# Per-head column tiles for the KV products, a sixteen-tile fold into the output weights, and a reordered opening, in an adaLN, linear-attention and SwiGLU block

## The chip, the cores and the metric

The kernel runs on one core of a Trainium2 chip. The metric is the device time of one execution in microseconds. A run also has a mean granted clock of the tensor engine (PE), 1.0 at full speed. All runs below count as fast (the single runs e7, e8 and e11 have no state), but in many of them the clock stood at half for some us near the start (3.4 or 6.8 us in the traces), which costs about 2 us (0.8 to 2.3 us in the traces). As the differences here are about as large, I use three readings: the medians, the runs with a clock of 1.000 alone ("full clock"), and distances between two instructions within a trace, which repeat to about 0.01 us.

## The reference, cut to what matters

```
S, D, H, Dh, F = 2048, 1024, 32, 32, 3584          # one sequence, bf16
mod = silu(c) @ w_mod -> sa, ca, ga, sb, cb, gb    # six rows of D
h   = layernorm(x) * (1 + ca) + sa
q, k, v = h @ wqkv                                 # 32 heads of 32
pq, pk  = phi(q), phi(k)                           # phi(t) = t+1 or exp(t), + 1e-6
kv = pk^T v  per head (32 x 32);  z = sum of pk per head
o  = (pq kv) / (pq z + 1e-6);     x = x + ga * (o @ wo)
h  = layernorm(x) * (1 + cb) + sb
x  = x + gb * ((silu(h @ w_gate) * (h @ w_up)) @ w_down)
```

## The kernel before

KV is the product `kv` of the reference, summed over all rows; a bank is one of the accumulators that PE writes. The sequence is cut into four chunks of 512 rows. Each chunk's key matmuls are eight groups of 8 matmuls (128x128 weights, 512 columns). After the first two key groups of a chunk come the KV products of the chunk before:

```python
def kv_phase(sc):
    for hg0 in range(0, HG, 3):                    # HG = 8 groups of four heads
        nh = min(3, HG - hg0)
        kvp = acc_b("kvp")                         # one bank for three groups
        ...
        for i in range(nh):
            for t in range(STC):                   # 4 tiles of 128 rows
                mm(kvv[:, i, :], lhsT=pks[sc][:, t, (hg0 + i) * P:(hg0 + i + 1) * P],
                   rhs=vs[sc][:, t, hg0 + i, 0:P + 1], start=(t == 0), stop=(t == STC - 1))
        ...                                        # added to kv_acc on VectorE
```

That is 128 keys by 128 values of four heads plus a column of ones, though only the four 32x32 blocks on the diagonal are wanted. A mask later zeroes the rest, eight transposes turn the masked groups, and sixteen matmuls, three after each query group, fold them into `wo`, so that attention and output projection become one product:

```python
        for hg, nb in wf[3 * (qc - 5):3 * (qc - 4)]:
            ps = acc_b("wf")
            w = wo[hg // 4][:, hg % 4, nb * NB:(nb + 1) * NB]
            mm(ps[:], lhsT=KVT[:, hg, :], rhs=w, start=True, stop=True)
            nc.scalar.copy(out=w, in_=ps[:])
```

Two chunks compute modulation rows directly behind `kv_phase`: `mod_rows`, 32 matmuls in four column tiles (32 weight columns each). The opening normalises the first chunk, transposes it on PE, and waits for the modulation weights `wme`. `keep_warm` issues dummy matmuls; `mod_block` computes shift or scale columns; `modulate` applies them on VectorE:

```python
        pe_transpose_tile(hT, xns[0], 0, DC)
        keep_warm(spare, 1)
        mod_block(0, 1, 0, 4)                      # scale
        pe_transpose_tile(hT, xns[1], 1, DC)
        keep_warm(spare, 1)
        pe_transpose_tile(hT, xns[2], 2, DC // 2)
        keep_warm(spare, 3)
        mod_block(0, 0, 0, 2)                      # shift, two columns
        for cc in (0, 1):
            modulate(hT, cc, ca1T, saT, 0, H)
        mod_block(0, 0, 2, 4)
        ...
        k_mms(0, gs, accs, 0, 3)                   # first key matmuls, six groups at once
        xn3 = ln1_norm(*ln1_stats(0, 3), dve=True) # fourth tile
        pe_transpose_tile(hT, xn3, 3, DC // 2)
        ...
        k_mms(0, gs7, accs7, 0, 4)                 # seventh key group
        mod_block(1, 0, 0, 2)
        for cc in (4, 5):
            modulate(hT, cc, ca1T, saT)
        k_mms(0, gs + gs7, accs + accs7, 4, 5)     # fifth chunk of the contraction
```

## Time and profile before

| reading | before |
|---|---|
| median (four runs beside the change) | 844.27 us (843.91 to 845.21) |
| profiled execution | 843.6 us, clock 1.000 |
| first key matmul to first value matmul | 17.08 us |
| first value matmul to first output projection | 151.66 us |
| PE time that one KV phase adds | 1.81 us, four of them |
| PE time that the fold matmuls add | 3.46 us |

The page of the kernel before: busy time of each engine, then PE's busy tenths and clock in 40 slices, then the chain of waits. (PEld is PE's weight loads, DVE is VectorE, ACT ScalarE, POOL GpSimd, SPq the queue of SyncE.)

```profile
PE 833.8 (99%) x4289; PEld 385.5 (46%) x4289; DVE 306.8 (36%) x599; ACT 176.2 (21%) x268; POOL 55.6 (7%) x163
...
PE   8999999999999999999999999999999999999998
...
PEclk9999999999999999999999999999999999999999
...
PE 98%; DMA 1%; SPq 0%; DVE 0%; issue 0%
```

PE is almost never free. The waits of the kernel before (what PE waited for, us in total, times, longest) name all there is, and all of it falls in the first 24 us:

```profile
PE mod_ps L98 <- DMA wme<-in_w_mod_dram: 1.8, 1, 1.8
PE acc L98 <- DVE sel L412: 1.2, 1, 1.2
PE acc L98 <- DVE hT L221: 0.7, 1, 0.7
PE mod_ps L98 <- DVE saT L267: 0.2, 1, 0.2
```

A matmul's shown duration includes its pipeline. What it costs PE is the distance between starts. The timeline of the kernel before (start, us, engine, line, matmul, array rows*columns, shape that streams, count; in brackets the idle time before and what ended it), KV and fold:

```profile
62.94 1.98 PE L98 MATMUL kvp<-v,pk 128*128 128x129 bf16 x32
64.75 10.52 PE L98 MATMUL acc<-wk,hT 128*128 128x512 bf16 x48
...
92.38 1.98 PE L98 MATMUL kvp<-v,pk 128*128 128x129 bf16 x32
94.29 1.91 PE L98 MATMUL modr<-wml,sc 128*32 128x512 bf16 x32
96.13 3.63 PE L98 MATMUL acc<-wk,hT 128*128 128x512 bf16 x16
...
162.23 0.63 PE L98 MATMUL den<-pq,Zden 128*32 128x128 bf16 x32
162.79 3.63 PE L98 MATMUL acc<-hT,wq 128*128 128x512 bf16 x16
166.25 0.81 PE L98 MATMUL wf<-wo,kvs 128*128 128x512 bf16 x3
166.90 1.89 PE L98 MATMUL acc<-hT,wq 128*128 128x512 bf16 x8
```

From 62.94 to 64.75 is the 1.81 us of a KV phase, 56.6 ns per matmul; three fold matmuls take 0.65 us, 216 ns each. The denominator matmuls (`den`, four column tiles) are the model for the new KV form: single starts there are 2 to 5 ns apart within a group of four, and the groups are 56 ns apart. The same timeline, the opening:

```profile
10.69 0.95 PE L98 MATMUL mod_ps<-scT,wme 128*128 128x1 bf16 x32 [1.83 <-DMA wme<-in_w_mod_dram]
...
13.55 0.55 PE L98 MATMUL mod_ps<-scT,wme 128*128 128x1 bf16 x16
14.36 0.54 PE L98 MATMUL mod_ps<-scT,wme 128*128 128x1 bf16 x16 [0.25 <-DVE saT L267]
14.78 4.06 PE L98 MATMUL acc<-wk,hT 128*128 128x512 bf16 x18
18.80 0.62 PE L101 MATMUL tp<-ident,xn 128*128 128x128 bf16 x8
...
23.46 2.55 PE L98 MATMUL acc<-wk,hT 128*128 128x512 bf16 x11 [0.71 <-DVE hT L221]
```

The first shift block at 13.55 us starts when its load lands (13.51 us), not when PE is ready.

### The profile page before, as it was taken

The page shows a single profiled execution, that of the slowest core. Times are in us where ns is not written, and L with a number is a line of the kernel's source. Part 1 is how long each engine was busy: PE and PEld are TensorE (multiplying, and loading weights), DVE is VectorE, ACT ScalarE, POOL GpSimd, SP SyncE. Part 2 cuts the span into 40 slices and gives each one's busy share as a digit, 9 for nine tenths or more (in the row PEclk, how much of TensorE's full clock was granted, in tenths as well). Part 3 has the DMA queues.
Part 4 walks back from the last instruction along what each step waited for, and adds up shares of the span by engine and source line. Part 5 has one row for each costly group of instructions (what it writes and reads, how often), then busy time and mean ns, then how long its engine had stood idle before and what let it go on. Part 6 is the DMA issues. An engine that isn't in the chain of part 4 may idle for free.

```text
span 841.5 us, 10528 instructions
## 1 busy us (share of the span) xinstructions
PE 833.8 (99%) x4289; PEld 385.5 (46%) x4289; DVE 306.8 (36%) x599; ACT 176.2 (21%) x268; POOL 55.6 (7%) x163
## 2 busy tenths in 40 slices
PE   8999999999999999999999999999999999999998
PEld 4444444544444444444444444444444444444444
DVE  5656563467523324432221344211124432111122
ACT  3355353354211111101111010111110101111000
POOL 3011010112050001100000010000001100000000
PEclk9999999999999999999999999999999999999999
DMA  9895770029998545528434073581504629720011
GB/s 304 308 248 122 232 188 1 2 52 250 348 236 251 193 145 175 154 70 257 151 100 150 25 233 106 178 260 52 198 1 131 182 69 315 238 66 1 17 60 50
DMA packets 127232, 128.74 MB, mean 153 GB/s; under 512 B 33616, under 2 KB 108880, under 8 KB 126672
## 3 DMA queue, kind: packets, MB, share of 16 engines
q1 hardware_dynamic: 123600, 115.36, 45.7%
q0 software_dynamic: 3584, 12.72, 4.9%
q8 instruction: 33, 0.54, 0.3%
q14 instruction: 15, 0.12, 0.1%
HBM read 108.01 MB, written 12.71 MB: 143 GB/s over the span
## 4 chain that ended last, share of the span: by engine, by line
PE 98%; DMA 1%; SPq 0%; DVE 0%; issue 0%
PE acc L98 89%; PE a_ps L98 7%; DMA wme<-in_w_mod_dram 1%; PE kvp L98 1%; PE modr L98 0%; PE wf L98 0%; PE mod_ps L98 0%; PE den L98 0%; SPq L120 0%; PE tp L101 0%; PE bcr L98 0%; SPq L131 0%; SPq L125 0%; DVE hT L221 0%; PE mcol L98 0%
## 5 line engine op out<-in xcount | busy, mean ns | idle before, releaser
L98 PE MATMUL acc<-h2T,wgu 128*128 128x512 bf16 x1792 | 387.6, 379 | 0.0
L98 PEld LDWEIGHTS <-wgu 128*128 128x128 bf16 x1792 | 175.0, 98 | 211.6
L98 PE MATMUL acc<-wd,gu 128*128 128x512 bf16 (+2 forms) x924 | 196.1, 373 | 0.0
L591 DVE TENSOR_TENSOR gu<-acc,e 128x512 bf16<-128x512 f32 x112 | 77.5, 692 | 299.3 <-PE acc L98 296.5
L590 ACT ACTIVATE e<-acc 128x512 f32<-128x512 f32 x112 | 66.9, 597 | 374.8 <-PE acc L98 374.8
L98 PEld LDWEIGHTS <-gu 128*128 128x128 bf16 x924 | 89.2, 98 | 104.6
L98 PEld LDWEIGHTS <-hT 128*128 128x128 bf16 x512 | 49.4, 98 | 60.3 <-DVE hT L221 1.3
L612 DVE TENSOR_TENSOR e<-acc,gb_bc 128x512 f32<-128x512 f32 (+2 forms) x33 | 22.3, 676 | 131.3 <-PE acc L98 131.3
L98 PE MATMUL acc<-wk,hT 128*128 128x512 bf16 x256 | 57.6, 379 | 0.7 <-DVE hT L221 0.7
L98 PE MATMUL a_ps<-wo,pq 128*128 128x512 bf16 x256 | 57.4, 379 | 0.0
L98 PE MATMUL acc<-hT,wq 128*128 128x512 bf16 x256 | 57.1, 379 | 0.0
L98 PE MATMUL acc<-wv,hT 128*128 128x512 bf16 x256 | 55.9, 379 | 0.0
L273 ACT ACTIVATE eb<-acc 128x512 bf16<-128x512 f32 x64 | 37.9, 596 | 63.4 <-PE acc L98 60.3
L218 ACT ACTIVATE xn<-x,nmr,rstd 128x1024 bf16<-128x1024 f32 x16 | 19.8, 1240 | 126.3 <-POOL nmr L216 126.3
L274 DVE TENSOR_SCALAR eb<-eb 128x512 bf16<-128x512 bf16 x64 | 18.4, 291 | 58.7 <-ACT eb L273 58.6
L98 PEld LDWEIGHTS <-pq 128*128 128x128 bf16 x256 | 25.0, 98 | 30.3
L98 PEld LDWEIGHTS <-wq 128*128 128x128 bf16 x256 | 24.9, 98 | 29.8
L559 POOL DMA_DIRECT2D x_scratch<-x x16 | 9.6, 600 | 418.6 <-DVE x L552 418.6
L552 DVE TENSOR_TENSOR x<-a_ps,x_sb 128x512 f32<-128x512 f32 x32 | 22.1, 692 | 8.2 <-PE a_ps L98 8.1
L202 POOL TENSOR_TENSOR rstd<-veps,neg_half 128x1 f32<-128x1 f32 x32 | 18.0, 562 | 86.0 <-DVE veps L200 75.2
L311 ACT CAST v<-acc 128x512 bf16<-128x512 f32 x32 | 18.3, 582 | 22.0 <-PE acc L98 22.0
L615 DVE TENSOR_TENSOR ob<-e,x1r 128x512 bf16<-128x512 f32 (+2 forms) x33 | 22.3, 675 | 1.0
(72 smaller groups left out, 276.9 us busy)
## 6 DMA issues: line engine op xcount, KB each, us to landing
wgu<-in_B_w_gate_dram SPq DMA_DIRECT2D x28, 1024.0 KB, 7.5
wgu<-in_B_w_up_dram SPq DMA_DIRECT2D x28, 1024.0 KB, 8.7
x_sb<-in_A_x_dram SPq DMA_DIRECT2D x32, 256.0 KB, 6.7
wml<-in_w_mod_dram SPq DMA_DIRECT2D x8, 1024.0 KB, 8.6
x_scratch<-x POOLq DMA_DIRECT2D x16, 512.0 KB, 3.1
x1r<-x_scratch SPq DMA_DIRECT2D x31, 256.0 KB, 2.9
wd<-in_B_w_down_dram SPq DMA_DIRECT2D x7, 1024.0 KB, 5.6
rbc<-rden_scratch POOLq DMA_DIRECT2D x16, 256.0 KB, 5.2
```

The lines of the kernel that those rows point to most:

```text
L98: return tc.keep_in_program_order(nc.tensor.matmul(out, lhsT=lhsT, rhs=rhs, start=start, stop=stop))
L202: nc.gpsimd.tensor_tensor(out=rstd[:, 0:n], in0=veps[:, 0:n], in1=neg_half[:].to_broadcast([P, n]), op=ALU.pow)
L218: nc.scalar.activation(out=dst, in_=src, func=ACT.Identity, bias=nmr[:], scale=rstd[:, 0:1])
L273: nc.scalar.activation(out=e[:], in_=acc, func=ACT.Exp)
L274: nc.vector.tensor_scalar(out=e[:], in0=e[:], scalar1=1.0, scalar2=PHI_EPS, op0=ALU.min, op1=ALU.add)
L311: nc.scalar.copy(out=v[:, t, nb * 4:(nb + 1) * 4, 0:P], in_=acc[:].rearrange("p (g e) -> p g e", e=P))
L552: nc.vector.tensor_tensor(out=x1[:, ns], in0=a_ps[:], in1=x_t[:, ns], op=ALU.add)
L559: nc.gpsimd.dma_start(out=x1_dram[st * P:(st + 1) * P, :], in_=x1[:])
L590: nc.scalar.activation(out=sg[:], in_=ps[0][:], func=ACT.Silu)
L591: gm = nc.vector.tensor_tensor(out=guT[sc][f // GPT][:, f % GPT, :], in0=ps[1][:], in1=sg[:], op=ALU.mult)
L612: nc.vector.tensor_tensor(out=yt, in0=y_ps, in1=gb_bc[:, ns], op=ALU.mult)
L615: nc.vector.tensor_tensor(out=ob, in0=yt, in1=x1r, op=ALU.add)
```

## The change

Its intent: compute only the 32x32 blocks that are wanted, four heads side by side as column tiles; keep KV unmasked and fold it in bursts of sixteen 32x32 tiles; move work into the waits of the opening; move the modulation rows two key groups behind KV. The core of the diff:

```diff
     def kv_phase(sc):
-        for hg0 in range(0, HG, 3):
-            ... # 32 matmuls, 128 weight columns, 129 moving columns
+        kvp = acc_b("kvp", (HG, 2, DH))
+        for hg in range(HG):
+            for t in range(STC):
+                for i in range(HPC):
+                    mm(kvp[i * DH:(i + 1) * DH, hg, :, :], lhsT=pks[sc][:, t, hg * P + i * DH:hg * P + (i + 1) * DH],
+                       rhs=v_ones(vs[sc], t * D + hg * P + i * DH), start=(t == 0), stop=(t == STC - 1))
+        ... # one accumulation on VectorE; v_ones: 32 value columns and 32 of ones
@@ opening
-        mod_block(0, 1, 0, 4)
         pe_transpose_tile(hT, xns[1], 1, DC)
         keep_warm(spare, 1)
+        mod_block(0, 1, 0, 4)
@@
-        ... # shift columns (0, 1), then (2, 3)
+        for lo, hi in ((0, 1), (1, 4)):
+            mod_block(0, 0, lo, hi)
+            for cc in range(lo, hi):
+                modulate(hT, cc, ca1T, saT, 0, H)
@@
-        k_mms(0, gs7, accs7, 0, 4)
+        k_mms(0, gs7, accs7, 0, 2)
         mod_block(1, 0, 0, 2)
         for cc in (4, 5):
             modulate(hT, cc, ca1T, saT)
+        k_mms(0, gs7, accs7, 2, 4)
@@ chunk loop
             kv_phase(sc - 1)
+            k_phase(sc, 2, 4)
             if sc >= 2:
                 row = mod_rows(blks)
-            k_phase(sc, 2, 4)
+            k_phase(sc, 4, 6)
@@ fold: two transposes instead of eight, wo loaded by eight DMAs in head order
+    def fold_wo(h, nb):
+        ns = slice(nb * NB, (nb + 1) * NB)
+        ps = [acc_b("wf") for _ in range(4)]
+        for i in range(HPC):
+            for g in range(4):
+                rs = slice(g * DH, (g + 1) * DH)
+                mm(ps[g][i * DH:(i + 1) * DH, :], lhsT=KVT[rs, h, i * DH:(i + 1) * DH], rhs=wo[h][rs, i, ns],
+                   start=True, stop=True)
+        for g in range(4):
+            (nc.scalar.copy if g % 2 == 0 else nc.vector.tensor_copy)(out=wo[h][:, g, ns], in_=ps[g][:])
+    q_phase(1, 4, 6)
+    fold_wo(0, 0)
+    q_phase(1, 6, 8)
+    fold_wo(0, 1)
+    q_phase(2, 0, 2)
+    fold_wo(1, 0)
+    q_phase(2, 2, 3)
+    fold_wo(1, 1)
... # cut: KVB, Zden and mask bookkeeping
```

## The prediction

> What bounds the kernel. The tensor engine: the page gives PE 833.8 of 841.5 us (99%), and the chain of waits is 98% PE, 89% of it 512-column matmuls that the change does not touch. The waits view shows 4 us of PE idle, all in the first 24 us. So only less PE work or a shorter opening counts; VectorE (36%), ScalarE (21%) and DMA have room.
>
> What the change does on the PE, from starts in the timeline:
>
> 1. KV products. Now four phases of 32 matmuls of 129 columns, 56.6 ns apart: 1.81 us each. After: 128 matmuls of 32 weight columns and 64 moving columns, in groups of four column tiles. The denominator matmuls here are such groups (128 moving columns): groups 56 ns apart over 96 in a row, and about 95 ns each to enter and leave this form. If a 64-column group takes about 30 ns, a phase is 32 x 30 + 190 = 1.15 us, 2.6 us less in four. The doubt is the weight load: the trace shows only that four loads of 32 columns fit in 56 ns. The Trainium skill ("TensorEngine Tiling (Array Packing)", Restrictions and Gotchas) says that column tiling excludes Fast Weight Load; if loads bind near 55 ns, a phase is about 1.95 us and the four lose 0.6 us. Weighed: 2.0 us saved.
>
> 2. Fold into wo. Now 16 matmuls 216 ns apart, 3.46 us. After: four bursts of sixteen tiles, each an estimated 95 + 50 + 216 + 95 = 0.45 us, 1.8 us in all. Given back: a burst wants all four banks of its pool. The last two are only one query group (1.73 us) apart, while the copies out, two of them behind the phi work on VectorE at about 0.69 us each, end some 2.6 us after the burst. I expect one PE stall of 0.5 to 0.9 us. Net 0.9 us saved.
>
> 3. Transposes of KV: eight become two, 6 x 56 ns = 0.34 us saved.
>
> 4. Modulation rows later: same work, same switches, nothing.
>
> 5. Opening. The first shift block starts when its 1 MB load lands (13.55 us), before and after; moving the scale block before it only fills idle time. Contracting one shift column first does not start K earlier (about 14.8 us as before), and the modulates end about 0.33 us later, so the fourth tile's transpose (18.80 us) slips to about 19.1 us. The split of the seventh group fills the 0.71 us wait before the fifth chunk: 0.43 us back. Net 0.1 us saved, give or take 0.4.
>
> Off the critical path: the eight smaller wo loads and fewer VectorE accumulations.
>
> Sum: 2.0 + 0.9 + 0.3 + 0.1 = 3.3 us, all critical. Predicted 841.1 us, range 838.9 to 843.5. Faster by over 2%: 0.01; within 2%: 0.98; slower by over 2%: 0.01.
>
> What would show it: KV starts in groups of four about 30 ns apart, phases of about 1.15 us (55 ns: step 1 wrong); wf bursts of about 0.45 us, and a PE wait of 0.5 to 0.9 us on a copy of wf at the last burst; the fourth tile's transposes at about 19.1 us with a PE wait of about 0.4 us, and the wait for hT before the fifth chunk down from 0.7 to about 0.4 us; the stages from gate_up on unchanged.
>
> What would make it wrong: weight loads or instruction issue binding the 32-column groups above 57 ns, which would make KV slower; mixing tile shapes costing more than 95 ns a switch; the sixteen tiles not running together; or late transposes of the last chunk stalling its key groups.

## The result, and the profile after

The changed kernel took 839.81 us (median of four runs, 839.35 to 842.05) against 844.27 us. The ratio is 0.9951 with a 95% interval of 0.9931 to 0.997; a ratio is the mean time of one kernel's fast runs over that of the other's of the same rounds, so not quite the ratio of the medians. 839.81 us lies in the predicted range.

The profiled execution was the slow one of the four, 842.05 us with a clock of 0.996; the others had 1.000 and 839.35 to 839.83 us. The page of the changed kernel:

```profile
PE 833.5 (99%) x4715; PEld 381.9 (45%) x4715; DVE 307.8 (37%) x597; ACT 171.9 (20%) x259; POOL 54.8 (7%) x158
...
PEclk8999999999999999999999999999999999999999
```

The windows view of it shows the reason for that 8. Columns: stretch, its length, then busy time and instructions of PE, weight loads, DVE, ACT and POOL, the granted clock, DMA share, GB/s.

```profile
14.00:20.00 6.00, 5.99 (x37) 2.56 (x37) 3.77 (x10) 0.00 (x0) 2.23 (x29) 0.50 1.11 348
```

The trace's clock records put the half-clock stretch at 13.66 to 20.49 us, over the first key matmuls. So the opening of this profile (its fourth transpose is at 21.41 us) says nothing about the change. Everything after it is clean. The timeline of the changed kernel:

```profile
65.19 1.22 PE L98 MATMUL kvp<-v,pk 128*32 128x64 bf16 x128
66.34 10.53 PE L98 MATMUL acc<-wk,hT 128*128 128x512 bf16 x48
...
94.07 1.22 PE L98 MATMUL kvp<-v,pk 128*32 128x64 bf16 x128
95.22 3.63 PE L98 MATMUL acc<-wk,hT 128*128 128x512 bf16 x16
98.78 1.91 PE L98 MATMUL modr<-wml,sc 128*32 128x512 bf16 x32
100.62 3.63 PE L98 MATMUL acc<-wk,hT 128*128 128x512 bf16 x16
...
173.78 0.43 PE L98 MATMUL wf<-wo,kvs 32*32 32x512 bf16 x16
174.15 1.90 PE L98 MATMUL acc<-hT,wq 128*128 128x512 bf16 x8
175.98 0.58 PE L98 MATMUL wf<-wo,kvs 32*32 32x512 bf16 x3
176.79 0.43 PE L98 MATMUL wf<-wo,kvs 32*32 32x512 bf16 x13 [0.23 <-DVE wo L532]
```

The KV phase starts to its successor in 1.15 us, plus about 0.1 us that now passes before it. The last fold burst breaks after three matmuls and waits for a VectorE copy. (The shown idle of 0.23 us counts from the modelled end of a matmul; between starts the break is 597 ns, plus 207 ns one matmul earlier.) The VectorE timeline has the two copies out of the third burst, the second of which ends at 176.74 us, and the phi work before them:

```profile
174.85 0.69 DVE L274 SCALAR_TENSOR_TENSOR pq<-acc,eb 128x512 bf16<-128x512 f32 x1
175.46 1.28 DVE L532 CAST wo<-wf 128x512 bf16<-128x512 f32 x2
```

The third burst began at 173.78 us, so the last of its banks came free 3 us later, and the last burst goes on at 176.79 us. The waits of the changed kernel show it too:

```profile
PE mod_ps L98 <- DMA wme<-in_w_mod_dram: 1.4, 2, 1.2
...
PE mod_ps L98 <- DVE saT L265: 0.2, 1, 0.2
PE acc L98 <- DVE hT L219: 0.2, 1, 0.2
PE wf L98 <- DVE wo L532: 0.2, 1, 0.2
```

What each part adds to PE, from the start of the matmul before it to the start of the matmul after it, less the 216 ns of the matmul before:

| part | before, us | after, us | saved, us | predicted, us |
|---|---|---|---|---|
| KV, four phases | 4 x 1.814 | 4 x 1.247 | 2.27 | 2.0 |
| fold matmuls | 3.455 | 3 x 0.459 + 1.261 | 0.82 | 0.9 |
| transposes of KV (with the switch after them) | 0.539 | 0.205 | 0.33 | 0.34 |
| first value matmul to first output projection (holds all three) | 151.66 | 148.33 | 3.34 | |
| last matmul's start to the end | 3.71 | 3.35 | 0.36 | none |

The parts add to 3.42 us against 3.34 for the stage. The 0.08 us between them lies one matmul later: after each tiled stretch of PE the gap between the first and the second ordinary matmul is 226 ns instead of 216, and the changed kernel has eight more such stretches (four of KV, four of the fold). The rest of the 4.46 us between the medians is the opening and the clock, for the experiments.

### The profile page after: what moved, and what is told of

The parts are those of the page before. It is cut to its first block, busy times and chain, and to the rows that moved or that the text cites. A ratio compares the mean times of both kernels' runs of the same rounds, so it can differ in the third digit from the quotient of the medians.

```text
span 839.9 us, 11373 instructions
## 1 busy us (share of the span) xinstructions
PE 833.5 (99%) x4715; PEld 381.9 (45%) x4715; DVE 307.8 (37%) x597; ACT 171.9 (20%) x259; POOL 54.8 (7%) x158
## 4 chain that ended last, share of the span: by engine, by line
PE 98%; DMA 1%; DVE 0%; SPq 0%; issue 0%; ACT 0%
PE acc L98 89%; PE a_ps L98 7%; DMA wme<-in_w_mod_dram 1%; PE kvp L98 1%; PE modr L98 0%; PE mod_ps L98 0%; PE den L98 0%; SPq L120 0%; DVE wo L532 0%; PE wf L98 0%; PE bcr L98 0%; DVE pq L274 0%; SPq L131 0%; ACT eb L271 0%; PE tp L101 0%
## 5 line engine op out<-in xcount | busy, mean ns | idle before, releaser
L98 PE MATMUL acc<-wk,hT 128*128 128x512 bf16 x256 | 61.0, 393 | 0.3 <-DVE hT L219 0.2
```

The source lines that it names most:

```text
L98: return tc.keep_in_program_order(nc.tensor.matmul(out, lhsT=lhsT, rhs=rhs, start=start, stop=stop))
```

## The experiments

Chips differ between groups of runs; each group has its own runs of the kernel before. Full-clock means are over runs with a clock of 1.000.

### e1: the changed kernel again

No edit.

> The changed kernel unaltered. The one profile of it had a granted clock of 0.5 from 13.7 to 20.5 us and took 842.05 us against 839.35 to 839.83 in the other runs. If that half-clock stretch belongs to some executions only, most runs here are 839.3 to 839.9 us and a profile without it shows what the opening gained: the fourth tile's transposes at about 19.0 us and the value matmuls starting at about 31.3 us (before: 31.86). If the changed opening always trips it, the stretch is there again and the runs spread to 842.

Measured: 841.8 us median (840.31 to 842.36, six runs), ratio 0.9966 (0.9952 to 0.9981). All six had a clock of 0.995 to 0.998, and no profile without the stretch was had. In the same rounds 6 of 11 runs of the kernel before had 0.996 to 0.998 (mean 845.4 us) and five had 1.000 (mean 843.35 us). So the stretch is not the change's alone: executions of both kernels have it. It costs about 2 us and moves medians by up to half of what was to be measured. From first value matmul to first output projection the trace has 148.33 us again.

### e2: KV column tiles alone

The kernel before with the new `v_phase` and `kv_phase`; the mask and the old fold read the narrow result:

```diff
-        nc.vector.tensor_tensor(out=KVZ[:, hs, :], in0=kv_acc[:, hs, 0:P], in1=kvmask..., op=ALU.mult)
+        for g in range(4 * h, 4 * h + 4):
+            nc.vector.tensor_tensor(out=KVZ[:, g, :].rearrange("p (i e) -> p i e", e=DH),
+                                    in0=kv_acc[:, g, 0:DH].unsqueeze(1).to_broadcast([P, HPC, DH]), ...)
```

> Only the per-head KV column tiles in the kernel before. Theory: a KV phase costs 1.25 us of PE instead of 1.81 (first read from the changed kernel's trace), so 4 x 0.57 = 2.3 us less, 842.0 us. Rival: most of the 4.5 us gain lies in the fold and the opening, and KV alone gives under 1 us, 843.5 us or more.

Measured: 842.02 us median, ratio 0.9971 (0.9953 to 0.9989); two full-clock runs, mean 840.38 us against 843.35. In the trace the stage takes 149.01 us, 2.66 us less than before: 2.27 us for the phases, as in the changed kernel, and 0.39 us more. The timeline of e2 shows where the extra comes from:

```profile
93.80 1.22 PE L98 MATMUL kvp<-v,pk 128*32 128x64 bf16 x128
94.83 1.92 PE L98 MATMUL modr<-wml,sc 128*32 128x512 bf16 x32
```

Here the modulation rows still follow KV directly. Both have four column tiles, and the first row matmul starts 8 ns after the last KV matmul. In the changed kernel PE leaves the form after KV and enters it again for the rows. So KV alone carries most of the gain, and moving the rows gave some of it away. e5 tests that.

### e3: the opening alone

The kernel before with the three edits of the opening, as in the diff above.

> Only the reordered opening in the kernel before. My prediction gave it 0.1 us. The stages of the changed kernel from the value matmuls to the first output projection add up to 3.3 us of the 4.5 us gained, so theory: the opening gives 0.8 to 1.2 us when the clock stays full, 843.2 us. Rival: it gives 0.1 us as predicted (844.1 us) and the rest comes from later stages. If the half-clock stretch comes from the opening, some runs here are some 2 us longer than the rest.

Measured: 844.58 us median, ratio 1.0002 (0.9986 to 1.0019); full clock 843.61 and 843.32 us against a mean of 843.35. The theory fell, the rival holds: the opening gives nothing that the time can show. This run's profile had full clock, so its opening can be read; timeline of e3:

```profile
13.71 0.35 PE L98 MATMUL mod_ps<-scT,wme 128*128 128x1 bf16 x8 [1.12 <-DMA wme<-in_w_mod_dram]
...
14.91 4.04 PE L98 MATMUL acc<-wk,hT 128*128 128x512 bf16 x17
19.24 0.62 PE L101 MATMUL tp<-ident,xn 128*128 128x128 bf16 x8 [0.29 <-DVE xn L212]
...
23.47 2.55 PE L98 MATMUL acc<-wk,hT 128*128 128x512 bf16 x11 [0.25 <-DVE hT L221]
```

The scale block moved into idle time, and the wait for the shift weights grew instead, to 1.12 us. From the first key matmul to the fourth transposes it is 4.33 us, 0.31 more than before; from there to the first value matmul 12.62, 0.44 less. Net: 16.95 instead of 17.08 us, the 0.1 us predicted. (e7 below has the whole changed opening at full clock in its trace, and 17.02 us there.) Four of the six runs had the half-clock stretch.

### e4: the last burst two query groups later

```diff
-    q_phase(2, 2, 3)
+    q_phase(2, 2, 4)
     fold_wo(1, 1)
...
-    q_phase(2, 3, 4)
```

> The changed kernel with the last fold burst two query groups after the one before it instead of one. Theory: the 0.8 us PE stall in that burst was a wait for the two VectorE copies that free its banks, so it goes and the kernel takes 839.0 us (0.8 us less than the changed kernel). Rival: the burst stalls for another reason (its weights or the array's form) and the time stays at 839.8 us.

Measured: 839.08 us median (838.24 to 840.02), ratio 0.9933; full clock 838.69 us (four runs). All four bursts now run whole, and the stage falls from 148.33 to 147.53 us, the 0.80 us expected. So the copies were the cause; in the changed kernel's trace, too, PE goes on 0.05 us after each of the two VectorE copies ends. But 0.30 us come back: from the first output projection to the first gate matmul the trace has 31.38 instead of 31.08 us. Two gaps there are 0.12 and 0.16 us longer than usual, while VectorE does the last two fold copies before the reciprocal multiply of the query tile. Its timeline in e4:

```profile
177.73 1.28 DVE L532 CAST wo<-wf 128x512 bf16<-128x512 f32 x2
178.93 2.49 DVE L410 TENSOR_TENSOR pq<-pq,rbc 128x1024 bf16<-128x1024 bf16 x4
```

The output projection that reads this tile starts at 179.89 us, before the multiply is done. e12 tests whether that is the cause.

### e5: the modulation rows directly behind KV again

```diff
# on e4
             kv_phase(sc - 1)
-            k_phase(sc, 2, 4)
             if sc >= 2:
                 row = mod_rows(blks)
-            k_phase(sc, 4, 6)
+            k_phase(sc, 2, 6)
```

> The kernel of e4 with the modulation rows directly behind the KV products again, as in the kernel before. Both are matmuls of four column tiles, and in e2 the rows started 8 ns after the last KV matmul (about 150 ns in the kernel before). Theory: two array form switches of about 95 ns go per stage, in two stages, so 0.38 us less than e4 between the first value matmul and the first output projection (147.14 us instead of 147.53), PE waits unchanged. Rival: the rows were moved because something they need (their weights, a bank) is late there, and a new PE wait takes the gain back.

Measured: 839.64 us median of four runs, all with a clock of 0.996 to 0.998, so its times can't be set against e4's. The trace can: the stage takes 147.10 us, 0.43 less than e4's 147.53, with no new wait. The theory holds (0.38 expected). Part 4 of the change, read alone, costs about 0.4 us; it only looks free against the kernel before, where KV had another form.

### e6: the opening filled with dummy matmuls

```diff
# on the changed kernel
         pe_transpose_tile(hT, xns[1], 1, DC)
-        keep_warm(spare, 1)
+        keep_warm(spare, 3)
...
-        keep_warm(spare, 3)
+        keep_warm(spare, 8)
         for lo, hi in ((0, 1), (1, 4)):
             mod_block(0, 0, lo, hi)
+            if lo == 0:
+                keep_warm(spare, 1)
```

> The changed kernel with 8 more dummy matmuls in the idle spots of the opening (2 before the first scale block, 5 before the first shift block, 1 between the shift blocks). Theory: the half-clock stretch of 3.4 or 6.8 us that starts at 13 to 16 us comes from low PE activity in the opening, so with the spots filled all runs have a mean granted clock of 1.000 and take 839.4 to 839.9 us; the kernel before still has it in about half its runs. Rival: the stretch does not depend on these idle spots, and about half of the runs or more keep a clock of 0.995 to 0.998 and take 840 to 842 us.

Measured: 839.5 us median, 839.46 to 840.12 over six runs, ratio 0.9946 (0.9933 to 0.996); five had 1.000, one 0.999. As runs with 0.999 take as long as full-clock runs (here 839.5 us), I count a run as having the stretch from 0.998 down: none of these six, against 7 of 11 runs of the kernel before and five of six with the unfilled changed opening (e5, e7, e8) in the same rounds. The windows of e6 over the stretch that stood at 0.50 in the changed kernel's profile:

```profile
7.00:14.00 7.00, 6.46 (x79) 3.83 (x79) 3.33 (x8) 3.52 (x4) 1.53 (x4) 1.00 1.06 358
14.00:20.00 6.00, 5.58 (x60) 2.96 (x58) 3.93 (x11) 0.00 (x0) 1.84 (x20) 1.00 1.11 342
```

PE is busy 6.46 of 7 us before 14 us, against 5.38 in the changed kernel's profile, and the clock stays. Over all groups, kernels with the filled opening (e6, e9, e10, e12) had the stretch in 1 of 22 runs, the kernel before in 20 of 42. That filling the idle spots takes the stretch away in nearly all runs is shown. That low PE activity is what brings it is the likely reading, but it is argued: the busy time from 7 to 14 us does not decide by itself, being 5.04 us in the kernel before and 5.18 in e7, whose profiles kept the clock, and 6.41 in e5, which lost it at 13.28 us. Which execution gets the stretch is not shown either. The Trainium skill ("TensorE: Matmul & The Clock Gate", Part 1) says that the clock gate judges PE by a free-running window of 3413 ns, and the stretches here last 3.41 or 6.83 us, once or twice that, which agrees. They also begin 6.8 or 10.2 us after the clock first rose to full, two or three such windows.

### e7 and e8: what limits the KV groups

Both give a wrong result: three of four KV matmuls stream 32 columns instead of 64 (e7), or load 16 weight columns instead of 32 (e8). (The comparison with the reference passed them within its tolerance, so it is no guard for this part.)

```diff
# e7, on the changed kernel
-                       rhs=v_ones(...)
+                       rhs=v_ones(...) if t == 0 else vs[sc][:, 32 value columns]   # into kvp[..., hg, 0, :]
# e8, on the changed kernel
+                    m = DH if t == 0 else DH // 2
-                    mm(kvp[i * DH:(i + 1) * DH, ...], lhsT=pks[...][32 columns], ...)
+                    mm(kvp[i * DH:i * DH + m, ...], lhsT=pks[...][m columns], ...)
```

> Wrong result on purpose: three of four KV matmuls stream 32 columns instead of 64. In the changed kernel the first nine groups of four are 28 to 29 ns apart and the rest 33 ns (8.3 ns per matmul). Theory: after the first 32 or so queued pairs the rate at which weight load and matmul pairs come in binds, not the stream: the spacing stays 8.3 ns per matmul and the phase stays at about 1.2 us. Rival: the 64 columns bind; then the groups fall to about 16 to 20 ns and a phase to about 0.8 us.

> Wrong result on purpose: three of four KV matmuls load 16 weight columns instead of 32. If the 8.3 ns per matmul is the weight load[...], the late groups of four fall from 33 to the stream's 29 ns and the phase by about 0.1 us. If it is the rate at which the instructions come in, nothing changes.

Measured, the distances in ns between the starts of successive KV matmuls of the first phase:

```
changed: 4 3 3 29 | 3 4 3 20 | ... (nine groups) ... | 8 8 9 8 | 8 10 7 8 | 9 8 8 9 ...   128 in 1024 ns
e7:      3 3 4 28 | 4 3 4 18 | 4 3 4 15 | ... (eight groups) ... | 8 9 8 8 | 11 8 9 8 ... 128 in 1023 ns
e8:      4 3 3 30 | 2 4 3 20 | ... (nine groups) ... | 8 8 11 3 | 9 8 9 8 ...             128 in 1022 ns
```

Neither half the stream nor half the weights shortens the phase. The first eight or nine groups come in bursts of four, about 30 ns per group (25 to 29 with 32 columns), then matmuls start every 8.3 ns one by one. So after the burst neither the length of the stream nor the number of weight columns binds; what is left is the rate at which pairs of weight load and matmul come in, or a fixed cost of each pair, whatever its size, which no run here separates from it. The Trainium skill ("TensorE: Matmul & The Clock Gate", spec table) gives the PE queue 64 entries, and the 32 to 36 pairs of the burst are 64 to 72 instructions, which fits pairs that waited there. That the rate is one of instruction supply is therefore argued from this, not measured.

### e11: the fold alone

The kernel before with only the fold, its two transposes and the eight `wo` loads; four small copies take the diagonal blocks of the wide KV:

```diff
+    for i in range(HPC):
+        rs = slice(i * DH, (i + 1) * DH)
+        nc.vector.tensor_copy(out=KVB[rs], in_=kv_acc[rs, :, rs])
```

> The kernel before with only the new fold and the two transposes (KV still 129 columns wide). Theory: from the first value matmul to the first output projection 0.82 + 0.33 = 1.15 us less than before (150.5 us against 151.66), including the stall of 0.8 us in the last burst. Rival: the fold gives nothing without the KV tiles, or the sum of the parts (2.66 for e2 less 0.38 for the rows, plus this) misses the 3.34 us of the whole change by over 0.2 us.

Measured: one run, 840.91 us at full clock against a mean of 842.89 for five full-clock runs of before. The stage takes 150.56 us, 1.10 us less (1.15 expected). The sum closes: e2's 2.66 less the rows' 0.43 plus 1.10 is 3.33 us, and the whole change has 3.34. The end is shorter too, 3.33 us after the last matmul's start instead of 3.71, so the shorter end belongs to this part.

### e9, e10: all repairs together, with the shift in pairs or the first alone

e9 is the changed kernel with e4, e5 and e6, and the shift blocks in pairs; e10 keeps the first shift alone.

```diff
# e9 against e10
-        for lo, hi in ((0, 1), (1, 4)):
+        for lo, hi in ((0, 2), (2, 4)):
```

> Everything together: the changed kernel with the last burst later (e4), the modulation rows directly behind KV (e5), the filled opening (e6), and the first shift blocks in pairs again as in the kernel before. Theory: 839.6 (e6) minus 0.8 (burst) minus 0.4 (rows) minus 0.3 (the fourth tile's statistics no longer wait for a third modulate) gives 838.1 us, clock 1.000 in nearly all runs. From the first key matmul to the first value matmul: 16.7 us instead of 17.0. Rival: the pairs make the first modulate late and K starts later by the same 0.3 us; then it ties with e10.

> As e9, but with the first shift contracted alone as in the change. Theory: 838.4 us, 0.3 us more than e9, with the wait of the fourth tile's transposes on its normalised tile at 0.3 to 0.4 us. Rival: no difference, or e10 the faster.

Measured: e9 838.81 us, e10 838.67 us median of five runs each, all at full clock; ratio 0.9947 for both, against full-clock runs of before of 842.89 us on average. Both missed their 838.1 and 838.4 us by 0.3 to 0.7, of which 0.30 is what e4 gave back (31.38 us from output projection to gate in both traces). In the traces the first key matmul to the first value matmul takes 16.71 us in e9 and 17.13 in e10, as the theory said, and e10 alone has the 0.36 us wait of the transposes. The times tie all the same (means 838.79 and 838.85); the start of the first key matmul moves with the landing of its loads, between 13.3 and 15.2 us in the traces, and a difference of 0.3 us does not get through that. The comparison of times is inconclusive.

### e12: three of four fold copies on ScalarE

```diff
# on e9
-            (nc.scalar.copy if g % 2 == 0 else nc.vector.tensor_copy)(out=wo[h][:, g, ns], in_=ps[g][:])
+            (nc.scalar.copy if g != 1 else nc.vector.tensor_copy)(out=wo[h][:, g, ns], in_=ps[g][:])
```

> e9 with three of the four copies of each fold burst on ScalarE instead of two. In e4 and e9 the later burst took its 0.8 us stall away, but two waits of 0.12 and 0.16 us came up in the first output projection, which needs the query tile that VectorE multiplies by the reciprocal after the last fold copies. Theory: VectorE is done 0.6 us sooner, both waits go, the stage from the first output projection to the first gate matmul falls from 31.38 to 31.08 us, and the kernel takes 838.5 us at full clock. Rival: ScalarE is now late with its copies or its exponentials and a new PE wait of 0.3 us or more appears between the bursts.

Measured: 838.29 us median (837.6 to 840.32, six runs), ratio 0.9933 (0.9917 to 0.995). Five runs at full clock have a mean of 838.07 us, against 843.31 for five of before in the same rounds, so 5.2 us less. First output projection to first gate matmul: 31.08 us. The waits of PE in e12, the whole list:

```profile
PE acc L98 <- DVE sel L412: 1.2, 1, 1.2
PE tp L101 <- ACT xn L216: 0.8, 1, 0.8
PE acc L98 <- DVE hT L219: 0.2, 1, 0.2
```

The theory holds. This version beats both kernels, and no PE wait is left after the opening.

## Why the prediction was right

The prediction was 841.1 us, 3.3 us less than the median quoted then; measured 839.81. Its mechanism holds, and its sum agrees with the distances in the traces; two things were left out, and that the blended KV figure came so close is partly luck.

- What binds: PE, as said; every stage gain above went straight into the stage's length.
- KV: predicted 2.0 us as a blend of a fast case (2.6) and a weight-load case (a loss of 0.6). The fast case was right in kind: 2.27 us. A group takes 33 ns over most of the phase instead of 30 (0.07 us in a phase), and entering and leaving take 0.22 us instead of 0.19, so a phase is 1.25 us and not 1.15. The fast case alone would have said 2.6, 0.3 us too much; the blend came closer because it averaged in a loss that did not occur, which is luck. The fear about weight loads, from the Trainium skill's "Column tiling disables: Fast Weight Load" ("TensorEngine Tiling (Array Packing)", Restrictions), did not come true: four loads of 32 columns fit in 33 ns, and halving them changed nothing (e8).
- Fold: predicted 0.9, measured 0.82. A burst adds 0.459 us (0.45 estimated), and the stall came in the burst that was named, for the reason that was named, with 0.80 us (0.5 to 0.9); e4 removed it by giving the copies time.
- Transposes: 0.33 of 0.34 us.
- Modulation rows: "same switches, nothing" is right against the kernel before. It missed that KV now has the rows' form, so that leaving them in place would have saved 0.43 us (e2, e5).
- Opening: 0.1 us predicted, 0.13 in e3's trace (0.06 in e7's) and no difference in time. The parts were right one by one: transposes at 19.24 us (19.1 predicted), with a wait of 0.29 (0.4), and the wait before the fifth chunk 0.25 us (0.4). The fourth transposes slip because VectorE does three modulates instead of two before the statistics.
- Left out, first: 0.36 us at the end. In every trace with eight `wo` loads the end comes 3.33 to 3.35 us after the last matmul's start, in every trace with two 3.70 to 3.71. SyncE there passes a row of semaphore waits about 61 ns apart, in the same order in every trace. The one that ends late, 2.38 us after that start, is the wait for the last output store. With two loads that store has the semaphore that comes third in the row, and seven waits follow; with eight it has the last but one, a single wait follows, and the six others are passed in time that is waited anyway. 6 x 61 ns is 0.37 us. The places in the row are read from the traces; that the number of DMAs decides which semaphore the store gets is argued, not tested.
- Left out, second: the half-clock stretch. The medians differ by 4.46 us, but the stages, the opening and the end give 3.34 + 0.1 + 0.36 = 3.8 us. At full clock it is 839.65 us (three runs) against 843.6 (the profiled execution of before, which is not one of its four), 3.95 us. The rest is probably how many runs of each kernel happened to have the stretch, which is luck; the clocks of the four runs of before are not on record, so it is not shown. The times alone can't confirm 3.8 us closely: at full clock and in the same rounds, e6 (the changed kernel with the filling) is 2.95 us under before (five runs against two), and e4 4.66 us, of which 0.5 is its own repair.

## What to carry to other kernels

Where the tensor engine is saturated, cost a change by distances between starts, and count how often the array changes its tile form: products of the same form belong side by side, at about 0.2 us for each leave and return. A burst that wants all banks of a pool needs the copies of the burst before it done, so look at the queue of the engine that copies, and at what those copies delay behind them. Before comparing kernels that differ by half a per cent, sort the runs by granted clock, and fill the idle spots of the opening with dummy matmuls.

## What the Trainium skill lacked or had wrong

- "TensorE: Matmul & The Clock Gate", Part 1 ("Wait — 56ns, not 53.3ns?"): starts never come less than about 25 ns apart, however small the matmul. For one-column matmuls of the whole array this agrees (25 ns), but it doesn't say that tiled forms are excepted: there starts are 2 to 5 ns apart within a group (about 4 ns by Part 3 of the page, which agrees), and 8.3 ns sustained over some 90 matmuls of 64 columns, which no page has.
- "TensorEngine Tiling (Array Packing)", Key Properties: says that a change of tiling mode drains the engine, but not what that costs. Here entering a tiled form cost about 93 ns (149 ns or 309 ns between starts where 56 or 216 is usual) and leaving the denominator form about 105 ns (151 ns to the next matmul, where 46 is usual to the next group); between KV and the modulation rows, which have the same form, it was 8 ns.
- The same page, Restrictions and Gotchas: column tiling excludes Fast Weight Load. No run here shows a cost of it: four loads of 32 columns in 33 ns, no faster with 16 columns.
- "TensorE: Matmul & The Clock Gate", Why this matters for your kernels: to avoid drops, no PE-idle gaps over about 3 us between bursts of matmuls. Here that is not enough: the longest single PE wait in the changed kernel's opening was 1.2 us, and the clock still went to half for 6.83 us. (Part 1 of the page tells of short idles doing this in another kernel, where PE cycles through accumulator banks.) No page says how much activity in a window keeps the clock, and the traces here do not settle it.
- No page that I read tells of the cost of the order of the final semaphore waits: 0.36 us here.
